# Retention in 192-token steps of three 64-token blocks, each block with its own running state

## The chip, the cores and the metric

One core of one Trainium2 chip. The metric is the device time of one launch in microseconds (us); the median of several runs counts.

## The reference

Attention without softmax and with a decay (retention), then a two-layer network. Batch 8 ("entries"), 8 heads, 576 tokens, head width 64; network width 512, hidden width 2048.

```python
scores = scale * np.matmul(q, k.transpose(0, 1, 3, 2))
gamma = 1.0 - 2.0 ** (-5.0 - np.arange(H))
Dmat = np.where(rel >= 0, gamma[:, None, None] ** rel[None, :, :], 0.0)   # rel = i - j
attn = np.matmul(scores * Dmat, v)
x = attn.transpose(0, 2, 1, 3).reshape(B * S, H * D)                     # 4608 x 512
h = x @ w_in
out = (h * (1.0 / (1.0 + np.exp(-1.702 * h)))) @ w_out
```

The decay factors into a power by the key's position, multiplied into v (`scale_v`), and one by the query's position (`gq`, applied when a result leaves PSUM). So a block of tokens needs three products: **scores** of its queries with its own keys, masked and multiplied with v (**values**); its keys with v, a 64x64 matrix for each head that is added to a running sum (**state**); and its queries with the sum of all earlier blocks (**inter**).

## The kernel before, in words

Each engine has one queue, written out by hand: `R.op` records operations in program order, and every operation waits for the last one that wrote or read the same buffer on another engine. Nothing is moved at run time, so an operation that waits holds up all that stand behind it in its queue.

**Dense work.** The 4608 tokens are 9 chunks of 512. `hidden(c, f)` is the first layer: four matmuls of 128x512 into one PSUM bank, then ACT applies the activation and writes `gT`. `project(c, r, g, bank)` is a quarter of the second layer for 128 tokens: four matmuls of 128x512; after the fourth quarter (g = 3) the bank is copied to `osb` by DVE (in chunk 0 by ACT) and stored by SP. Such a group of four matmuls is called a unit here. `hidden_half` is a unit of eight matmuls of 128x256. From chunk 3 on, `region(c)` alternates units of `hidden(c)` and `project(c - 1)`.

**Retention.** Entry 0 has a special path at the start. Entries 1 to 7 go in steps of 128 tokens (five in an entry, the last of 64). `burst(n)` puts one step between two units: PE computes values, state and inter of step n - 1 and, between their two parts, the scores of step n; then DVE masks the scores (`mask_s`, L426), moves the result to `xT` (`evac_o`, L573), and adds the state in `zacc` and casts it to `zq` (`evac_z`, L547 to L554), which the next burst reads. All these matmuls use quarters of the array: 64 rows and 64 columns, so four run at a time. The second part (`part(1)`) waits for PE's own first part (`own=first`).

**Inputs.** POOL issues loads in the order written (`load`, `load_entry`); k and v of heads 4 to 7 are shifted by 64 tokens (`load_shifted`). Three entries have room. `scale_v` on DVE multiplies v in place. q and k are turned (head width to partitions): steps up to 9 by PE and ACT (`turn`: eight transposes into bank `psW`, then `evac_t`), later ones by DMA transposes that SP issues three steps ahead (`dma_turn`), in one queue with the output stores.

**PSUM, eight banks.** `psS` two banks for scores; `psV` two banks for values, inter and state; `psW` for turns, and later for every second projection; `psU` for the other projections; `psH` two banks for `hidden`.

## Time and profile before

| what | value |
|---|---|
| runs (median; lowest, highest) | 307.18 us; 306.03, 308.02 |
| profiled execution, first to last instruction | 304.7 us |
| TensorE (PE) busy | 297.3 us, 98% |
| VectorE (DVE), ScalarE (ACT), GpSimd (POOL) busy | 147.8, 108.8, 154.2 us |
| granted TensorE clock | 1.00 |
| PE matmuls | 3175 recorded |

A launch takes about 2.5 us more than the span from first to last instruction (307.18 against 304.7). Busy shares are unions over each engine's instructions; PE's matmuls are pipelined, so the busy share says where PE has work and not that it runs at its peak.

### The profile page before, as it was taken

The page shows a single profiled execution, that of the slowest core. Times are in us where ns is not written, and L with a number is a line of the kernel's source. Part 1 is how long each engine was busy: PE and PEld are TensorE (multiplying, and loading weights), DVE is VectorE, ACT ScalarE, POOL GpSimd, SP SyncE. Part 2 cuts the span into 40 slices and gives each one's busy share as a digit, 9 for nine tenths or more (in the row PEclk, how much of TensorE's full clock was granted, in tenths as well). Part 3 has the DMA queues.
Part 4 walks back from the last instruction along what each step waited for, and adds up shares of the span by engine and source line. Part 5 has one row for each costly group of instructions (what it writes and reads, how often), then busy time and mean ns, then how long its engine had stood idle before and what let it go on. Part 6 is the DMA issues. An engine that isn't in the chain of part 4 may idle for free.

```text
span 304.7 us, 7234 instructions
## 1 busy us (share of the span) xinstructions
PE 297.3 (98%) x3175; PEld 151.0 (50%) x3175; DVE 147.8 (48%) x246; ACT 108.8 (36%) x183; POOL 154.2 (51%) x208
## 2 busy tenths in 40 slices
PE   7899999999999999999999999999999999999996
PEld 3454545885444444444444444444444444444444
DVE  6689837554767833545546433444364431100012
ACT  8666524661035423322333223323233333333300
POOL 8998999999999999999850000000000000000000
PEclk9999999999999999999999999999999999999999
DMA  9999999999999999999999933213231000001012
GB/s 69 152 195 196 176 168 200 155 145 129 158 194 175 132 156 164 169 161 173 174 169 163 133 84 95 58 38 86 71 80 37 34 37 34 34 37 66 37 54 86
DMA packets 154303, 35.61 MB, mean 117 GB/s; under 512 B 144928, under 2 KB 149792, under 8 KB 154272
## 3 DMA queue, kind: packets, MB, share of 16 engines
q0 software_dynamic: 118384, 18.36, 87.3%
q1 hardware_dynamic: 35888, 16.79, 29.3%
q8 instruction: 25, 0.41, 0.6%
q14 instruction: 6, 0.05, 0.1%
HBM read 36.70 MB, written 9.44 MB: 151 GB/s over the span
## 4 chain that ended last, share of the span: by engine, by line
PE 83%; POOL 9%; DMA 3%; DVE 3%; issue 1%; POOLq 0%
PE psH L634 31%; PE psU L687 18%; PE psW L687 16%; PE psV L445 4%; DMA st_k<-in_k_dram 3%; PE psH L687 3%; PE psH L671 3%; POOL st_k L211 2%; POOL st_q L198 2%; PE psS L404 2%; PE psU L671 1%; PE psV L464 1%; POOL st_k L198 1%; POOL st_v L198 1%; PE psV L457 1%; POOL st_v L211 1%
## 5 line engine op out<-in xcount | busy, mean ns | idle before, releaser
L639 ACT ACTIVATE gT<-psH 128x512 bf16<-128x512 f32 x121 | 72.2, 597 | 153.8 <-PE psH L634 153.8
L634 PE MATMUL psH<-xT,w_in_sb 128*128 128x512 bf16 x484 | 118.1, 379 | 0.0
L426 DVE TENSOR_TENSOR sm<-psS,mask 128x1024 bf16<-128x1024 f32 (+1 forms) x39 | 43.5, 1114 | 85.1 <-PE psS L404 80.8
L634 PEld LDWEIGHTS psH<-xT,w_in_sb 128*128 128x128 bf16 x484 | 45.8, 98 | 54.9 <-ACT gT L639 1.6
L211 POOL DMA_DIRECT2D st_k<-in_k_dram x70 | 69.2, 1250 | 1.6 <-PE psV L464 0.9
L211 POOL DMA_DIRECT2D st_v<-in_v_dram x70 | 68.1, 1240 | 0.0
L687 PE MATMUL psU<-w_out_sb,gT 128*128 128x512 bf16 x256 | 62.7, 379 | 0.0
L687 PE MATMUL psW<-w_out_sb,gT 128*128 128x512 bf16 x224 | 54.8, 379 | 0.0
L198 POOL DMA_DIRECT2D st_q<-in_q_dram x40 | 52.7, 1317 | 0.2 <-issue 0.2
L687 PEld LDWEIGHTS psU<-w_out_sb,gT 128*128 128x128 bf16 x256 | 24.2, 98 | 28.0
L687 PEld LDWEIGHTS psW<-w_out_sb,gT 128*128 128x128 bf16 x224 | 21.3, 98 | 25.0
L343 DVE TENSOR_TENSOR st_v<-st_v,vfac 128x512 bf16<-128x512 bf16 x37 | 25.2, 680 | 3.1 <-DMA st_v<-in_v_dram 3.1
L699 DVE COPY osb<-psU 128x512 f32<-128x512 f32 x15 | 10.3, 687 | 28.6 <-PE psU L687 28.6
L573 DVE TENSOR_TENSOR xT<-psV,gq 128x512 bf16<-128x512 f32 (+1 forms) x35 | 21.9, 627 | 4.2 <-PE psV L464 4.2
L699 DVE COPY osb<-psW 128x512 f32<-128x512 f32 x14 | 9.6, 689 | 21.7 <-PE psW L687 21.7
L687 PE MATMUL psH<-w_out_sb,gT 128*128 128x512 bf16 x80 | 18.7, 379 | 0.0
L445 PE MATMUL psV<-sm,st_v 64*64 64x64 bf16 (+1 forms) x504 | 17.5, 214 | 0.3
L445 PEld LDWEIGHTS psV<-sm,st_v 64*64 64x64 bf16 x504 | 9.1, 104 | 15.7 <-issue 12.1
L372 ACT ACTIVATE qk<-psW 128x1024 bf16<-128x1024 bf16 x10 | 10.2, 1023 | 9.2 <-PE psW L366 9.2
L457 PE MATMUL psV<-st_v,st_k 64*64 64x64 bf16 x448 | 13.0, 192 | 0.0
L464 PE MATMUL psV<-qk,zq 64*64 64x128 bf16 (+1 forms) x224 | 12.6, 215 | 0.1
L687 PEld LDWEIGHTS psH<-w_out_sb,gT 128*128 128x128 bf16 x80 | 7.6, 98 | 8.5
(108 smaller groups left out, 212.7 us busy)
## 6 DMA issues: line engine op xcount, KB each, us to landing
out_dram<-osb SPq DMA_DIRECT2D x35, 256.0 KB, 2.4
st_q<-in_q_dram POOLq DMA_DIRECT2D x32, 128.0 KB, 17.5
st_k<-in_k_dram POOLq DMA_DIRECT2D x57, 64.0 KB, 17.2
st_v<-in_v_dram POOLq DMA_DIRECT2D x57, 64.0 KB, 17.2
w_out_sb<-in_moe_w_out_dram POOLq DMA_DIRECT2D x4, 512.0 KB, 11.9
w_in_sb<-in_moe_w_in_dram POOLq DMA_DIRECT2D x3, 512.0 KB, 7.8
st_k<-in_k_dram POOLq DMA_DIRECT2D x4, 128.0 KB, 4.2
st_v<-in_v_dram POOLq DMA_DIRECT2D x4, 128.0 KB, 4.6
```

Source lines behind the costliest of these rows:

```text
L198: R.op("POOL", lambda e, d=d, s=s: e.dma_start(d, s), w=[(nm, sl, c)], dma=(nm, sl, c))
L211: R.op("POOL", lambda e: [e.dma_start(d, s) for d, s in parts], w=[(nm, sl, c)], dma=(nm, sl, c), parts=2)
L343: R.op(eng, lambda e: e.tensor_tensor(t, t, f, ALU.mult), r=[("vfac", min(b, 1))], w=[("v", sl, c)])
L426: R.op("DVE", lambda e: e.tensor_tensor(o, i, m, ALU.mult), r=[("mask", 0), ("mask", 1)] if b else mask3_keys if c == 3 else [("mask", 0)] ...
L445: i = e.matmul(psV[half(t), u, 128 * j + 64 * last : 128 * j + N], st_v[rows, sl, cc, 64 * h : 64 * h + 64], s[rows, j, 2 * t + u, 64 * la ...
L457: i = e.matmul(psV[half(j), u, 256 + 64 * t : 320 + 64 * t], st_k[rows, sl, cc, hs], st_v[rows, sl, cc, hs], start=False, stop=False, skip ...
L464: i = e.matmul(psV[half(t), u, 128 * j : 128 * j + N], zq[(c - 1) % 2][half(j), 2 * u + t, :], qk[n % NQK][half(j), 0, 2 * u + t, 0:N], st ...
L573: R.op("DVE", lambda e: e.tensor_tensor(xT[:, :, t0 : t0 + N].rearrange("p (u j) n -> p u j n", u=2), psV[:, :, 0:256].rearrange("p u (j n ...
L634: i = e.matmul(bank.ap(), w_in_sb[:, a, 128 * f : 128 * f + 128], xT[:, a, 512 * c : 512 * c + 512], start=(a == 0), stop=(a == 3))
L639: R.op("ACT", lambda e: e.activation(gT[c % 2][:, f, :], bank.ap(), AF.Gelu_apprx_sigmoid), w=[("gT", c % 2, f)], ps=[key])
L687: i = e.matmul(bank, gT[c % 2][:, f, 128 * r : 128 * r + 128], w_out_sb[:, f, :], start=(f == 0), stop=(f == NF - 1))
L699: R.op("DVE", lambda e: e.tensor_copy(osb[m].ap(), bank), w=[("osb", m)], ps=[key])
```

## The change

Entries 1 to 7 now go in steps of 192 tokens, three in an entry, m = 0 to 20 (entry 1 + m//3). A step is three blocks g of 64 tokens, and each block has a running state of its own (`zw[g]`). So no scores between different blocks are computed within a step: scores, values, state and inter are all products of 64 by 64 by 64, eight for each block and kind (no inter in an entry's first block, no state in its last).

- `burst(m_out, m_in)` does values and inter of step m_out and state and scores of step m_in. Its order on PE: phase_x (values of even blocks, half of inter), state of blocks 1 and 0, scores, state of block 2, phase_y (the rest). One wait on PE's own earlier work is kept in it.
- On DVE: `evac_wide` (768 elements), `mask_wide` (768), the state sums one block after the other (`state_wide`: 256 elements for an even block, two of 128 for an odd one), and one cast of all three to `zw`.
- PSUM: the five banks `psA` hold scores and parts of the state (0, 1), values and inter and parts of the state (2, 3), and turns and parts of the state (4, the former `psW`). The projections lose `psW`: they use `psU` alone in the regions.
- k is turned together with q of the same chunk; the first keys' own turn is gone. `qk` has six buffers instead of four, and SP turns six chunks ahead.
- Loads: k is no longer loaded a chunk ahead of q; the third and fourth parts of `w_out` stand at other places; entry b + 3 is loaded chunk by chunk as the steps of entry b finish.
- The order of units and bursts from the first projection to chunk 3 is written anew; in the regions a burst stands behind the second unit of a group of eight.

```diff
+            def score(e):
+                for blk, g in enumerate(blocks(m_in)):
+                    for t in range(2):
+                        for u in range(2):
+                            c, r = place(g, u)
...
+                            for j in range(2):
+                                i = e.matmul(psA[half(r), j, 64 * x : 64 * x + 64],
+                                             qk[n % NQK][half(j), 1, 2 * u + t, half(r)],
+                                             q_of(m_in, g, j, u, t), ...
...
+            if m_out is not None:
+                ro = [("sm", si(m_out)), "zw"] + [("v", b % NST, c) for c in cs] + queries(m_out)
...
+                done = R.op("PE", phase_x, r=ro, ps=["O", "Z"])
+            if m_in is not None:
...
+                before = R.op("PE", state_a, r=rs, ps=["S", "Z", "W"])
+                R.op("PE", score, r=rq, ps=["S"])
+                if m_in % 3 < 2:
+                    R.op("PE", lambda e: state(e, 2, (2,) if fresh else ()), r=rs,
+                         ps=["O", "W"], own=None if fresh else before)
+                    done = None
+                else:
+                    done = done and before
+            if m_out is not None:
...
+                R.op("PE", phase_y, r=ro, ps=["O", "Z"], own=done)
+                evac_wide(m_out)
+            if m_in is not None:
+                mask_wide(m_in)
+                state_wide(m_in)
...
+        def state_wide(m):
+            keys = ["S", "W", "Z", "O"]
...
+                if g % 2 == 0:
...
+                    add(src, blk, 0, 256, g == 0)
+                else:
+                    add(flat[:, at0 : at0 + 128], blk, 0, 128, False)
+                    add(flat[:, at1 : at1 + 128], blk, 128, 256, False)
+            R.op("DVE", lambda e: e.tensor_copy(z, zacc[:, 0 : len(gs), :]),
+                 r=[("zacc", x) for x in range(len(gs))], w=["zw"])
...
-        load(1, 0, "kq")
-        load(1, 1, "k")
+        load(1, 0)
         load_w_out(2)
-        load(1, 0, "v")
+        load(1, 1, "qk")
         load_w_out(3)
-        load_entry(1, 1)
+        load(1, 1, "v")
+        load_entry(1, 2)
         load_entry(2)
...
+        def step(m, into=True):
+            b, i = 1 + m // 3, m % 3
+            burst(m, m + 1 if into and m + 1 < NWIDE else None)
+            for c in ((0,), (1, 2), (3, 4))[i]:
+                n = NC * b + c + NQK
+                if PE_TURNS <= n < NSTEP:
+                    turn_dma(n)
+                if b + NST < B:
+                    load(b + NST, c)
+
+        def scale(m):
+            for c in ((0, 1), (2, 3), (4,))[m % 3]:
+                scale_v(NC * (1 + m // 3) + c)
...
+        run([unit_o(0, r, g, wide_banks[(1, 2, 0)[r]], "ACT") for g in range(4) for r in range(3)]
+            + [unit_o(0, 3, g, wide_banks[1], "ACT") for g in range(4)],
+            {1: [(tail_turn,)], 3: [(intra, 4)], 5: [(tail_out,)], 6: [(turn, 5)],
+             8: [(scale_v, 5)], 12: [(turn, 6), (scale_v, 6)], 14: [(burst, None, 0)]})
+        step(0, False)
+        turn_dma(10)
         hcount[0] = 16
+        run([unit_h(1, 0, f) for f in range(0, NF, 2)],
+            {0: [(turn, 7), (scale_v, 7)], 2: [(turn, 8), (scale_v, 8)],
+             5: [(burst, None, 1)], 6: [(turn, 9), (scale_v, 9)]})
+        run([unit_o(1, r, g, wide_banks[(1, 2)[r]]) for r in range(2) for g in range(4)],
+            {0: [(step, 1)], 4: [(step, 2, False)], 5: [(scale, 3)]})
+        run([unit_h(1, 1, f) for f in range(0, NF, 2)],
+            {3: [(burst, None, 3)], 5: [(scale, 4)]})
+        run([unit_o(1, r, g, wide_banks[(0, 1)[r - 2]]) for r in range(2, 4) for g in range(4)],
+            {1: [(step, 3)], 3: [(scale, 5)], 5: [(step, 4)]})
+        hcount[0] = 0
+        run([lambda f=f: hidden(2, f, 3) for f in range(NF)],
+            {1: [(scale, 6)], 3: [(step, 5)], 5: [(scale, 7)], 8: [(step, 6)],
+             10: [(scale, 8)], 13: [(step, 7)]})
...
+        hcount[0] = 0
+        scale(9)
         for c in range(3, NCH):
             region(c)
```

`run(units, between)` records the units in order, and behind unit i what `between[i]` names. `wide_banks` are psU, psH0, psH1 and a bank of psA, in this order; `hidden` rotates over psH0, psH1 and, with a third argument of 3, psU. In the new `region` each group of eight units is two hidden, four projections and two hidden in the order h0, o0, o1, h1, o2, o3, h2, h3; a burst follows o0, and `scale` follows h2.

## The prediction

> **What bounds the kernel now.** I read the page's head first, then its chain of waits.

> ```profile
> span 304.7 us, 7234 instructions
> ...
> PE 297.3 (98%) x3175; PEld 151.0 (50%) x3175; DVE 147.8 (48%) x246; ACT 108.8 (36%) x183; POOL 154.2 (51%) x208
> ...
> PE 83%; POOL 9%; DMA 3%; DVE 3%; issue 1%; POOLq 0%
> ```

> PE sets the end; the POOL and DMA shares lie before 47 us, where loads come in. So I count PE: work taken off it counts in full, and so does every new wait in its queue. A span of 304.7 belongs to a time of about 307.2, so 2.5 us lie around it, and I leave these as they are. A measurement here tells 1% (3.1 us) from no change.

> The timeline of PE around one steady burst (start, duration, line, shape, count) prices PE's work:

> ```profile
> 206.38 1.03 PE L634 MATMUL psH<-xT,w_in_sb 128*128 128x512 bf16 x4
> 207.34 0.31 PE L445 MATMUL psV<-sm,st_v 64*64 64x128 bf16 x8
> 207.48 0.23 PE L457 MATMUL psV<-st_v,st_k 64*64 64x64 bf16 x8
> 207.54 0.23 PE L464 MATMUL psV<-qk,zq 64*64 64x128 bf16 x4
> 207.59 0.34 PE L404 MATMUL psS<-qk 64*64 64x128 bf16 x16
> 207.84 0.26 PE L445 MATMUL psV<-sm,st_v 64*64 64x64 bf16 x8
> 207.92 0.23 PE L457 MATMUL psV<-st_v,st_k 64*64 64x64 bf16 x8
> 207.99 0.23 PE L464 MATMUL psV<-qk,zq 64*64 64x128 bf16 x4
> 208.15 0.39 PE L687 MATMUL psW<-w_out_sb,gT 128*128 128x512 bf16 x1
> ```

> Starts count, since durations overlap. A unit takes 0.864, so the burst could begin at 207.24 and holds PE until 208.15: 0.90. Eight 64-wide matmuls (L457) take 0.06: four run at once, 0.030 a round. A 128-wide round takes 0.055. Around the rounds lie 0.09 going in, 0.025 more after a start or wait, and 0.12 going out beyond the last round. The wait on PE's own part 1 ends about 0.28 after that part's last start.

> VectorE's operations by shape (count | busy, mean ns) price the other side:

> ```profile
> L426 DVE TENSOR_TENSOR sm<-psS,mask 128x1024 bf16<-128x1024 f32 x31 | 37.9, 1223 | 69.5 <-PE psS L404 65.9 <-PE psS L393 3.6
> L343 DVE TENSOR_TENSOR st_v<-st_v,vfac 128x512 bf16<-128x512 bf16 x37 | 25.2, 680 | 3.1 <-DMA st_v<-in_v_dram 3.1
> L573 DVE TENSOR_TENSOR xT<-psV,gq 128x512 bf16<-128x512 f32 x28 | 19.0, 680 | 0.0
> ...
> L552 DVE CAST zq<-zacc 128x256 bf16<-128x256 f32 x21 | 8.0, 380 | 0.7
> L549 DVE TENSOR_TENSOR zacc<-zacc,psV 128x256 f32<-128x256 f32 x14 | 5.7, 409 | 0.0
> ```

> Size sets them: 0.15 plus 1.04 ns an element. So 768 elements take 0.95 and 128 take 0.28. The cast's undisturbed duration is 0.293; for 768 I take 0.55, between that and three times it. An independent operation starts 0.09 before the one ahead ends, a dependent one 0.04 after. DVE starts 0.26 after PE's last start, and PE 0.06 after DVE's end: a `scale_v` that began at 44.78 and took 0.69 let the burst start at 45.53.

> **Part by part: PE's work.** Taken gap by gap between units, PE's small matmuls and its waits from the first projection (32.36) to the end sum to 34.2, 1.6 of it waits for loads. An entry's five bursts cost 0.79 + 0.90 + 0.90 + 0.90 + 0.61 = 4.1.

> After, a full burst has 6 rounds of values, 6 of scores, 6 of inter (4 if m_out is an entry's first step) and 6 of state (4 if m_in is its last): 22 rounds where m_out is the first or second step, 24 where it is the third. That is 0.09 + 22 x 0.030 + 0.05 + 0.07 (what the scores don't hide of the own wait) + 0.12 = 0.99, or 1.05. Eighteen such bursts: 13 x 0.99 + 5 x 1.05 = 18.1. The order breaks three joints: `burst(None, m)` for 0, 1 and 3 has 12 rounds (0.60 each, 1.8); `burst(m, None)` for 0, 2 and 20 has nothing to hide the own wait, 0.81 + 0.88 + 0.88 = 2.6. Turns 4 to 9 at 0.45, and the tail's scores (0.32) and values (0.48) as now: 3.5. Sum 26.0 against 34.2: **a gain of 8.2**. Units are the same in number. A longer run of 64-wide rounds than four has no row; its bounds are 0.028 (the closest pair) and 0.053 (a first pair after a stop). I take 0.030, by the unbroken pairs.

> [...]

> **Part by part: new waits of PE.** DVE's chain from a burst, where each operation depends on the last: mask 0.87, state sums 0.45 for an even block (256) and 0.64 for an odd one (2 x 128), cast 0.55: 2.96 after an entry's first step, 3.15 after its second, 2.4 after its third (two blocks). With `evac_wide` ahead 0.86 more: 3.8 to 4.0. PE must read `zw` at the next phase_x. In a region 6.9 of units lie between, and nothing waits. Between 32 and 113 us it is otherwise:

> - *Loads.* The third `w_out` part lands when it did, but its project comes 1.0 earlier: 0.2. The fourth now stands behind all of q and k of chunk 1 and lands about 1.1 later than its 42.1 (the trace's landing time); PE wants it at 42.0: 1.2. Together 1.4.
> - *burst(0, None)* has one unit (0.86) between it and step 0's scores, whose chain needs 2.96 + 0.3: 2.2 of wait. Hidden there before by three units and more.
> - *hidden_half(1)* then needs that burst's `evac_wide`: 0.26 + 0.95 + 0.06, less the usual exit: 1.1.
> - *turn(9)* writes `psW`, where parts of step 1's state lie, so it waits for DVE's last sum: ready 3.3 after `burst(None, 1)` began, PE there at 1.5: 1.8.
> - *step(4)* comes 3.45 after step 3, whose chain takes 4.0; then the copy of `osb` and `scale_v` of the last chunk (0.6 each) stand in DVE's queue ahead of what its state needs: 1.7.
> - *hidden(2, 0)* takes psH0, which the projection just finished; its copy stands behind step 4's chain (3.24) and the 0.69 of its own: PE is ready 1.7 after the burst, the bank 4.0: 2.3.
> - *steps 6 and 7* wait for `scale_v` behind the chain: 0.6 + 0.2. *hidden_half(1, 1)*'s second bank: 0.1.
> - *hidden(3, 0)* takes psH0 straight after hidden(2, 15) used it, so the activation (597 ns by L639) shows: 0.8.
> - *DMA turns.* These land 7 to 9 us after issue (page: 7.2 and 7.6 in the median). SP issues chunks 22 and 23 only after step 7 and q's landing at 113.7; step 9 wants them near 123, step 8 chunk 21 near 115: 1.4, bounds 0 and 3.

> Sum **13.6**. What stands behind these waits in other queues doesn't reach PE: the loads of entries 5 to 7 land about 10 us or more ahead of need by the landing times of before, and `osb` has three buffers for SP's stores.

> Net 13.6 - 8.2 = +5.4: span 310.1, time **312.6**.

> **The rivals.**

> *A. VectorE's chain is much shorter (not slower).* If the sums and the cast overlap more than rows of 256 and above show, five waits shrink together: burst(0, None), turn(9), step 4, psH0 and step 6, each by what the chain loses. So 1 us off every chain is worth some 4.5 to 5, and past 1.1 us the change wins: at 1.3 us the time is 306.7. For: L552's shortest, and the 128-wide sums have no row. Against: L426, L573 and L549 lie on one line to 1%.

> *B. More waits of the same kind.* The new order has some thirty places where PE waits for DVE or a DMA; two more of 1.2, or casts disturbed as L552's mean against 0.293 shows, give 315.2. For: L552 took 0.5 to 0.78 six times between 97 and 142. Against: regions have slack of 2 us and more.

> *C. Rounds paced by weight loads.* At 0.053 a round, 23 ns x 20 rounds x 21 steps = 9.7 more: 322. For: first pairs. Against: all unbroken ones. [...]

> *D. The change wins outright.* If PE waits nowhere for DVE, 8.2 less 2.8 for loads and turns: 301.8. Against it: each wait above follows from an operation's place in its queue.

> **How the numbers follow.** Forecast (309 to 314.5) 0.56, A 0.18, B 0.16, C 0.06, D 0.04. The range reaches down to where A ends the change's loss, 306.5, leaving out D and a part of A, and up to 317.5, leaving out C and little of B. Faster by over 1% (under 304.1): D and A's tail, 0.05. Within 1% (to 310.3): the rest of A and the lower edge of the forecast, 0.19. Slower: 0.76.

> **What would show it.** Right: a steady burst at about 1.0 with three in an entry; PE idle before `burst(0, None)`, turn(9), step 4 and hidden(2, 0), put down to DVE; the regions from chunk 3 shorter by some 4.7 (17.9 of bursts against 13.2), the stretch ahead of them longer by about 10. Wrong: steady bursts over 1.2 (C), chains under 3 us with `evac_wide` (A), or PE waits in the regions.

## The result and the profile after

The change makes the kernel slower: 318.41 us against 307.02 in runs on the same chip, a ratio of 1.0357 (1.0312 to 1.0401). The direction is as forecast; the size is twice the forecast 5.4 and the time lies 0.9 above the upper end of the range.

| | before | after |
|---|---|---|
| median (lowest, highest), us | 307.02 (306.03, 308.02) | 318.41 (316.45, 319.01) |
| profiled execution: time, span | 307.18, 304.7 | 318.88, 316.6 |
| the last 832 large weight loads (the regions, from behind chunk 3's first step on), first to last | 193.2 | 188.8 |
| start of the first of these loads | 108.5 | 124.8 |
| mean granted clock | 1.00 | 0.984 |

The rows on weight loads are read from the trace: large means 128x128, and both kernels have 832 of them from these points on. The regions are 4.4 shorter, close to the forecast 4.7. The stretch ahead, which has step 8 in it, is 16.3 longer where 10.1 was forecast. The whole error lies there.

The page of the changed kernel, head and chain:

```profile
span 316.6 us, 7664 instructions
...
PE 292.9 (93%) x3358; PEld 149.1 (47%) x3395; DVE 148.8 (47%) x274; ACT 108.3 (34%) x182; POOL 155.5 (49%) x208
...
PEclk9999998799997999999999999999999999999999
...
PE 76%; DVE 11%; DMA 5%; POOL 4%; issue 3%; POOLq 0%
```

PE's share fell from 98% to 93%, and DVE took 11% of the chain where it had 3%: new waits on DVE. Nothing in this says why the clock has two dips (slices 7, 8 and 13 of 40, each 7.9 us), nor what "issue 3%" is, which was 1%.

The chain of DVE was forecast well. Its groups by shape (count | busy, mean ns | idle before):

```profile
L623 DVE TENSOR_TENSOR xT<-psA,gq 128x768 bf16<-128x768 f32 x21 | 20.1, 958 | 52.9 <-PE psA L552 52.9
L634 DVE TENSOR_TENSOR sm<-psA,maskw 128x768 bf16<-128x768 f32 x21 | 19.9, 949 | 16.7 <-PE psA L564 16.7
...
L647 DVE TENSOR_TENSOR zacc<-zacc,psA 128x128 f32<-128x128 f32 x56 | 16.0, 286 | 1.7
...
L663 DVE CAST zw<-zacc 128x768 bf16<-128x768 f32 x14 | 8.5, 611 | 0.5
```

958 and 949 ns answer to the 0.95 used, 286 to 0.28, and 611 to 0.55. The timeline of PE around one steady burst of 22 rounds (start, duration, line, shape, count):

```profile
198.00 1.03 PE L730 MATMUL psU<-w_out_sb,gT 128*128 128x512 bf16 x4
198.96 0.32 PE L536 MATMUL psA<-sm,st_v 64*64 64x64 bf16 x16
...
199.35 0.38 PE L578 MATMUL psA<-qk 64*64 64x64 bf16 x24
...
199.71 0.23 PE L552 MATMUL psA<-qk,zw 64*64 64x64 bf16 x8
...
200.10 0.81 PE L730 MATMUL psU<-w_out_sb,gT 128*128 128x512 bf16 x3 [0.16 <-issue]
```

Here is a trap. From 198.86, where the unit ends, to 200.10 are 1.24 us. But the unit that follows shows x3: its first matmul has no record. Its weight loads are all in the trace. With the 0.216 of that matmul taken off, the burst costs 1.02 us; over the regions the mean is 1.013. Likewise a burst of 24 rounds reads 1.393 and costs 1.177. The "issue" gaps of 0.16 to 0.22 after bursts (2.2 us for psU L730 below) are such holes and no wait: 37 matmuls lack a record.

PE's waits (engine, buffer, line <- what ended the wait: us in all, times, longest):

```profile
PE psA L536 <- DVE zw L663: 2.8, 2, 2.2
PE psA L578 <- issue: 2.5, 2, 1.8
PE psU L730 <- issue: 2.2, 14, 0.2
PE psH L677 <- DVE osb L742: 2.1, 1, 2.1
...
PE psA L365 <- DVE zacc L647: 1.6, 1, 1.6
...
PE psH L714 <- DVE xT L623: 1.1, 1, 1.1
```

They are the forecast ones: step 0 and step 6 (L536: 2.2 and 0.6), `hidden(2, 0)` behind the copy of `osb` (L677), `turn(9)` behind the state sums (L365), `hidden_half(1)` behind `evac_wide` (L714). One is not: L578, the scores, stopped twice for 2.5 in all with nothing to release it.

Term by term, measured gap by gap between units of PE:

| term of the sum | forecast | measured |
|---|---|---|
| gain of bursts, turns and tail | -8.2 | -7.3 |
| loads of `w_out` | 1.4 | 0.6 |
| `burst(0, None)`, step 0 and `hidden_half(1)` | 3.3 | 3.3 |
| `turn(9)` | 1.8 | 1.8 |
| step 4 | 1.7 | 1.7 |
| `hidden(2, 0)` | 2.3 | 2.3 |
| steps 6 and 7, `scale_v` | 0.8 | 0.8 |
| `hidden(3, 0)`, second half bank | 0.9 | 1.0 |
| DMA turns | 1.4 | 0.1 |
| halved clock | none | 4.6 |
| stops inside steps 7 and 8 | none | 2.9 |
| net | +5.4 | +11.8 |

The last number stands against 11.9 between the spans. Six rows of waits agree to 0.1. Two rows that the sum lacked are 7.5 together, and make the miss. Of the other errors, 0.9 too much gain and 2.1 too much for loads and turns partly cancel, which is luck.

### The profile page after: what moved, and what is told of

It reads as the page before. It is cut to its first block, busy times and chain, and to the rows that moved or that the text cites. A ratio compares the mean times of both kernels' runs of the same rounds, so it can differ in the third digit from the quotient of the medians.

```text
span 316.6 us, 7664 instructions
## 1 busy us (share of the span) xinstructions
PE 292.9 (93%) x3358; PEld 149.1 (47%) x3395; DVE 148.8 (47%) x274; ACT 108.3 (34%) x182; POOL 155.5 (49%) x208
## 4 chain that ended last, share of the span: by engine, by line
PE 76%; DVE 11%; DMA 5%; POOL 4%; issue 3%; POOLq 0%
PE psU L730 28%; PE psH L677 27%; PE psH L730 6%; DMA w_out_sb<-in_moe_w_out_dram 4%; PE psH L714 3%; DVE zacc L647 3%; PE psA L536 2%; PE psA L578 2%; DVE sm L634 2%; DVE xT L623 2%; PE psU L714 2%; DMA st_k<-in_k_dram 2%; PE psA L564 1%; POOL st_q L208 1%; PE psA L552 1%
## 5 line engine op out<-in xcount | busy, mean ns | idle before, releaser
L677 PE MATMUL psH<-xT,w_in_sb 128*128 128x512 bf16 x453 | 110.3, 383 | 3.7 <-DVE osb L742 2.1
L730 PE MATMUL psU<-w_out_sb,gT 128*128 128x512 bf16 x416 | 100.9, 379 | 2.3 <-issue 2.2
L677 PEld LDWEIGHTS psH<-xT,w_in_sb 128*128 128x128 bf16 x464 | 43.5, 98 | 60.2 <-ACT gT L682 7.3
L730 PEld LDWEIGHTS psU<-w_out_sb,gT 128*128 128x128 bf16 x432 | 41.1, 98 | 47.8
L742 DVE COPY osb<-psU 128x512 f32<-128x512 f32 x26 | 17.9, 688 | 72.4 <-PE psU L730 72.4
L623 DVE TENSOR_TENSOR xT<-psA,gq 128x768 bf16<-128x768 f32 x21 | 20.1, 958 | 52.9 <-PE psA L552 52.9
L730 PE MATMUL psH<-w_out_sb,gT 128*128 128x512 bf16 x120 | 28.7, 379 | 1.4 <-issue 0.8
L634 DVE TENSOR_TENSOR sm<-psA,maskw 128x768 bf16<-128x768 f32 x21 | 19.9, 949 | 16.7 <-PE psA L564 16.7
L647 DVE TENSOR_TENSOR zacc<-zacc,psA 128x128 f32<-128x128 f32 (+1 forms) x77 | 24.8, 322 | 2.2
L730 PEld LDWEIGHTS psH<-w_out_sb,gT 128*128 128x128 bf16 x128 | 11.9, 98 | 14.0 <-DMA w_out_sb<-in_moe_w_out_dram 0.9
L536 PE MATMUL psA<-sm,st_v 64*64 64x64 bf16 x504 | 11.9, 197 | 3.0 <-DVE zw L663 2.8
L371 ACT ACTIVATE qk<-psA 128x1024 bf16<-128x1024 bf16 x10 | 10.2, 1023 | 11.7 <-PE psA L365 11.7
L714 PE MATMUL psH<-xT,w_in_sb 128*128 128x256 bf16 x88 | 12.8, 298 | 1.1 <-DVE xT L623 1.1
L536 PEld LDWEIGHTS psA<-sm,st_v 64*64 64x64 bf16 x504 | 7.6, 107 | 12.4 <-issue 6.8
L663 DVE CAST zw<-zacc 128x768 bf16<-128x768 f32 (+1 forms) x21 | 11.6, 550 | 0.7
## 6 DMA issues: line engine op xcount, KB each, us to landing
st_k<-in_k_dram POOLq DMA_DIRECT2D x57, 64.0 KB, 11.6
```

The source lines that it names most:

```text
L536: i = e.matmul(psA[half(t), 2 + u, at : at + 64], rows_of(st_v, m_out, g, u, 4 * u + 2 * t + j), smw[si(m_out)][half(r), j, 2 * blk + t, : ...
L623: R.op("DVE", lambda e: e.tensor_tensor(xT[:, :, t0 : t0 + 192].rearrange("p (u j) n -> p u j n", u=2), psA[:, 2:4, 0:384].rearrange("p u ...
L634: R.op("DVE", lambda e: e.tensor_tensor(o, i, k, ALU.mult), r=["maskw"], w=[("sm", si(m))], ps=["S"])
L647: R.op("DVE", lambda e: e.tensor_tensor(to, was, src, ALU.add), r=[("zacc", (blk - 1) % 3)], w=[("zacc", blk)], ps=keys)
L677: i = e.matmul(bank.ap(), w_in_sb[:, a, 128 * f : 128 * f + 128], xT[:, a, 512 * c : 512 * c + 512], start=(a == 0), stop=(a == 3))
L714: m = e.matmul(bank[:, 256 * i : 256 * i + 256], w_in_sb[:, a, 128 * (f + i) : 128 * (f + i) + 128], xT[:, a, a0 : a0 + 256], start=(a == ...
```

## Two theories

**K, the clock.** The trace's windows of PE, cut at the times at which the granted clock changes (window, its length, PE busy (count), clock, DMA share, GB/s):

```profile
49.41:52.82 3.41, 1.03 (x42) 1.00 1.79 242
52.82:56.23 3.41, 2.45 (x16) 0.50 2.12 196
...
93.78:97.19 3.41, 1.27 (x7) 1.00 1.79 142
97.19:100.61 3.42, 3.42 (x10) 0.50 1.64 186
```

All changes stand on one grid of 3.413 us. In the window before each fall PE was busy for only 1.03 and 1.27 us (2.38 and 2.14 idle): the waits at step 0 and at `hidden(2, 0)`. The next window runs at 0.50, and a 128x512 matmul takes 0.427 there instead of 0.216. A halved window loses 1.71 us where PE works through all of it. In the first of the three windows PE stood for 0.96, so the three lose 4.6, matmul by matmul. The four runs of the changed kernel fit: clocks of 0.984, 0.989, 0.995 and 0.984 went with spans of 316.6, 315.3, 314.5 and 316.9, so three, two, one and three windows, some 1.1 for each window more. K says: a window with enough idle time in it halves the next.

**F, the program.** The stop inside step 8, in the timeline:

```profile
120.78 0.35 PE L578 MATMUL psA<-qk 64*64 64x64 bf16 x20
122.90 0.22 PE L578 MATMUL psA<-qk 64*64 64x64 bf16 x4 [1.77 <-issue]
```

The scores stop after 20 of 24, in the middle of one operation whose inputs all came together. Counting PE's instructions in the trace (a matmul is two, a weight load and a matmul; an instruction that only waits for a semaphore is one), the two stops stand behind instruction 2754 and 3010, 256 apart. The trace has a queue q8, "instruction", with 16 KB packets at 112.54 to 113.79 and 120.07 to 121.24; PE went on 1.5 and 1.7 after their ends. F says: PE's program arrives in blocks of 256 instructions, a block comes some 7 us after the one before was entered while POOL's loads run (entered at 108.46, 115.26 and 122.90: 6.8 and 7.6 apart), and PE stops where it is faster. A burst of 22 rounds is 176 instructions in 0.8 us; before, 112. The trace has 6854 instructions of PE instead of 6405.

The rivals to K and F stand in the expectations.

## Experiments on the clock

**e4_idle**: the kernel before with stalls in it, each a chain of dependent copies on DVE that PE waits for; nothing else changes.

```diff
+        def stall(count):
+            last = R.q["PE"][-1]
+            for _ in range(count):
+                R.op("DVE", lambda e: e.tensor_copy(
+                    posi[:, 0:2, :], psS[:, 0, 0:2, :]),
+                    w=["stall"], ps=["S"], own=last)
...
+        stalls = {(7, 5): 4, (7, 13): 5, (7, 21): 4, (7, 29): 5,
+                  (8, 2): 3, (8, 10): 4, (8, 18): 5, (8, 26): 6}
...
+                if g == 1:
+                    stall((7, 5, 4)[r])
```

`stalls` gives the region, the unit in it and the number of copies; the last two lines are for the tail, and every large unit now waits for "stall".

> The kernel before, with eleven places between 240 and 310 us at which PE waits for a chain of 3 to 7 dependent copies on VectorE (256 elements each), so for an estimated 1.7, 2.1, 2.6, 3.1 or 3.5 us; the work is the same otherwise. Theory K: a grid of 3.41 us windows runs on its own; the clock falls to 0.50 at the end of a window of which PE was idle for some 2.5 us or more, and stays for one window if PE is then busy. So waits of 1.7 never do it, waits of 2.1 and 2.6 only where they lie inside one window, and 3.1 and 3.5 about half the time or more; every stretch at 0.50 is a multiple of 3.41 us and starts on the grid. Rival L: no fall at all, since nothing else is loaded there. Rival M: the length of the single wait decides (over 2.2 us always, below never).

The span was 345.3 and the mean clock 0.965. Two of the places, windows of PE:

```profile
258.84:262.25 3.41, 2.34 (x11) 1.00 0.00 0
262.25:265.66 3.41, 1.99 (x10) 1.00 0.20 77
...
296.38:299.80 3.42, 1.14 (x6) 1.00 0.00 0
299.80:303.21 3.41, 3.19 (x9) 0.50 0.00 0
```

A wait of 2.5 us from 260.6 on fell on both sides of a window's edge, 1.07 and 1.42 of idle, and the clock stayed. The third row had 2.28 idle in one window (3.42 less 1.14), and the next window ran at 0.50. So the length of the wait did not decide here, 2.5 without a fall, but its share of one window, 2.28 with one. Over the traces of all kernels of this study the clock fell 20 times while PE still had work. The window before had 2.06 to 3.41 us in which PE neither multiplied nor loaded weights, and no window with 1.93 or less was followed by a fall. The clock came back after windows with 0.53 or less, and not after those with 0.83 or more. So K stands, with a lower limit than the 2.5 that it was given, and the rivals L and M fall.

**e1_fill**: the changed kernel with 34 matmuls on a spent operand put into five of its waits; 94 small matmuls at the start shift the program's blocks.

```diff
-        fill(14)
...
+        small(94)
+        fill(11)
...
+        fill(9, *wide_banks[0])
         step(0, False)
+        fill(4, *wide_banks[0])
...
-             5: [(burst, None, 1)], 6: [(turn, 9), (scale_v, 9)]})
+             5: [(burst, None, 1)], 6: [(fill, 7, *wide_banks[0]), (turn, 9), (scale_v, 9)]})
...
-            {1: [(step, 3)], 3: [(scale, 5)], 5: [(step, 4)]})
+            {1: [(step, 3)], 3: [(scale, 5)], 5: [(fill, 5, *wide_banks[2]), (step, 4)]})
+        fill(9, *wide_banks[2])
```

> The changed kernel, with matmuls on zeros (34 of 128x512, 0.216 us each) put into PE's five longest waits between 49 and 97 us: 9 before step 0, 4 behind it, 7 before turn(9), 5 before step 4, 9 before hidden(2, 0). The waits themselves stay. At the start 3 of 14 such matmuls are replaced by 94 small ones, so that the later instructions keep their places in blocks of 256. Theory K: the 5.1 us that the halved clock took (three stretches of 3.41 us at 0.50) come from PE's idleness in these waits; the clock stays at 1.00, the span falls from 316.6 to about 311.5 and the time by 3 to 5 us. Rival L: the clock falls for another reason, such as the load of all engines and transfers together at these places; 0.50 shows again and the time stays within 1 us or grows.

The clock was 1.000 and the time did not move: 318.15, ratio 1.0351 (1.0306 to 1.0395). So K is right on what halves the clock, and wrong that curing it gains 3 to 5 us here. Of the 4.6, 4.2 came back as other delays, gap by gap: 2.0 at step 2 (1.5 of it a new stop, from 73.06 to 74.54), 0.6 of longer waiting at step 0, 0.7 of small matmuls at the start, 0.6 of waits ahead of 43 us, 0.3 at step 4. Part of this is F's.

## Experiments on the program's blocks

**e7_code**: the kernel before with 640 small matmuls ahead of region 3, while loads run, and 640 behind region 8, when they are over.

```diff
+        small(640, (psH[0], psH[1]), [("H", 0), ("H", 1)])
         for c in range(3, NCH):
             region(c)
+        small(640, (psH[0], psH[1]), [("H", 0), ("H", 1)])
```

> The kernel before, with two runs of 640 small matmuls on zeros (64 by 64 by 64, four at a time, 1280 instructions of PE each): one ahead of chunk 3's region at about 108 us, while the loads run, and one behind the last region at about 302 us, where only the output's stores are left. At 0.0317 us a round of four each run takes 5.1 us. Theory F: PE gets its program in blocks of 256 instructions, one asked for when the one before is begun. At 108 us each block needs 6.8 to 7.6 us, so the run takes some 30 to 38 us with a gap of 6 us or so at every 256th instruction; at 302 us, with fetches of 1 us and 1.5 behind them, 2.5 to 2.8 a block and 12 to 14 us in all. Rival T: no gaps, 5 to 6 us each, and the same in both places.

The timeline of both places (128 small matmuls are 256 instructions):

```profile
114.96 1.92 PE L899 MATMUL psH<-idle 64*64 64x64 bf16 x128 [6.44 <-issue]
121.98 1.92 PE L899 MATMUL psH<-idle 64*64 64x64 bf16 x128 [5.10 <-issue]
...
331.26 1.93 PE L899 MATMUL psH<-idle 64*64 64x64 bf16 x128 [2.77 <-issue]
334.72 1.92 PE L899 MATMUL psH<-idle 64*64 64x64 bf16 x128 [1.53 <-issue]
```

128 matmuls take 1.9 us in five of these blocks and 1.2 in the one at 327.26 (the mean clock of the run was 0.947), and then PE stands for 5.1 to 6.4 us early and 1.5 to 2.8 late. A block takes 7.0 to 8.1 us while the loads run and 3.2 to 4.0 when they are over, more than the 2.5 to 2.8 expected there. F stands: this is the cost of a block measured by itself.

**e2_shift**: the changed kernel with 62 small matmuls for two large ones at the start, so that every later block ends 120 instructions earlier in the work.

```diff
-        fill(14)
...
+        small(62)
+        fill(12)
```

> The changed kernel with 62 small matmuls on zeros at its start in place of 2 of 14 large ones, where PE only keeps busy: every later PE instruction lies about 120 places further in the program, nothing else differs. Theory F: the stalls inside the scores of steps 7 and 8 (0.91 and 1.96 us) are waits for the next block of 256 instructions, which in the changed kernel are 256 places apart and each end some 1.5 us after a 16 KB packet of the instruction queue. With block ends 120 places earlier in the code these fall among whole units, and both stalls go: the span is 2.5 to 2.9 us shorter if the clock does what it did. Rival T: those stalls are the scores' own, waiting for DMA turns of chunks 19 to 21; they stay where they are, and so does the time.

The timeline, at step 1 and at step 8:

```profile
70.58 0.22 PE L536 MATMUL psA<-sm,st_v 64*64 64x64 bf16 x3 [1.32 <-issue]
...
122.23 0.38 PE L578 MATMUL psA<-qk 64*64 64x64 bf16 x24
```

Step 8's scores are whole now; with step 7's they give 2.9 back. A new stop came inside step 1, behind instruction 1474, which is 5 x 256 ahead of 2754. That the stops of steps 7 and 8 go was forecast, the sum was not: with the new stop, 0.7 more at step 4 and 1.0 lost by 43 us, most of it to the small matmuls, the time is 318.54, ratio 1.0374 (1.0325 to 1.0423). A shift of the blocks moves the stops.

**e9_no_loads**: the changed kernel without the loads of entries 4 to 7.

```diff
-                if b + NST < B:
+                if b + NST < 4:
```

> The changed kernel without the loads of entries 4 to 7 (POOL's issues from about 85 to 160 us): those entries are computed from the data of entries 1 to 3, the order and number of all other operations stay. Theory F, with the loads as what makes PE's code late: from some 95 us on the blocks of 256 instructions come in 3 to 4 us as they do at the end of the kernel, the stalls inside the scores of steps 7 and 8 (0.9 and 1.9) are gone, and nothing else on PE gets longer: span some 2.8 below 316.6, or below what the granted clock of this run makes of it. If the delay comes from the fetches themselves, or from the DMA turns, which stay, the blocks still take 7 us and the stalls remain.

One execution took 313.33, with a span of 311.3 and a clock of 0.995. Step 8 in the timeline:

```profile
117.58 0.38 PE L578 MATMUL psA<-qk 64*64 64x64 bf16 x24
```

Both stops are gone with the program as it was: steps 7 and 8 cost 1.24 and 1.18, and PE entered blocks 5.7 us apart without a stop. The packets of these two blocks began 0.7 and 0.9 us after the block before was entered; in the changed kernel it was 4.1 and 4.8. So what the loads delay is the start of the packet, and the stops come from the loads and the density of bursts together; the DMA turns, which stay, are not the cause. One window was halved instead of three, 1.7 lost instead of 4.6. These two, 2.9 and 2.9, less 0.5 that this run was behind before the first wait already, are the 5.3 between the spans.

## Experiments on the order

These keep the change and write its order anew, to take away the waits of the table. Numbers stand for "behind unit i", as in the change.

**e5_order**: eight buffers for `qk`, turns and `scale_v` earlier, `hidden(2, 0)` begins in psH1.

```diff
-NQK = 6
+NQK = 8
...
-            {0: [(turn, 7), (scale_v, 7)], 2: [(turn, 8), (scale_v, 8)],
-             5: [(burst, None, 1)], 6: [(turn, 9), (scale_v, 9)]})
+            {1: [(turn, 8), (scale_v, 8)], 3: [(turn, 9)],
+             5: [(burst, None, 1)], 6: [(scale_v, 9)]})
...
-            {3: [(burst, None, 3)], 5: [(scale, 4)]})
+            {2: [(burst, None, 3)], 4: [(scale, 5)], 5: [(scale, 6)]})
...
-        hcount[0] = 0
+        hcount[0] = 1
```

> The changed kernel with its steps and the bursts' work as they are, but another order between 40 and 125 us and eight buffers qk: burst(None, 0) two units earlier, turn(7) ahead of the first half unit, turn(9) ahead of burst(None, 1), step 3 one unit earlier, scale_v of the later steps ahead of the chains, hidden(2, f) beginning with psH1. By the prediction's terms this takes away most of burst(0, None) (1.7 of 2.2), 0.45 of the half unit's 1.1, turn(9)'s 1.8, step 4's 1.7, hidden(2, 0)'s 2.3, hidden(3, 0)'s 0.9 and step 6's 0.6: 9.4 us, and by theory K the clock stays at 1.00, 5.1 more. Theory F sets a bound: with the steps closer together, each block of 256 instructions still takes 6.8 to 7.6 us to come while the loads run, so stalls of 1 to 4 us show at block ends in steps 5 to 8. Sum: span 303 to 306, time about 305 to 308.5, as fast as before. Without F 302 or less; if the waits only move elsewhere, 312 or more.

312.96, ratio 1.018 (1.0131 to 1.023). The waits of `turn(9)`, `hidden(2, 0)` and `hidden(3, 0)` are gone. My order had a fault of its own: `scale(6)` waited in DVE's queue for a v that landed at 84.4, and step 4 behind it waited 2.5. Block ends took 1.0 and 2.6 in steps 7 and 8.

**e6_order2**: steps earlier still, so that each has units on both sides.

```diff
-             8: [(scale_v, 5)], 12: [(turn, 6), (scale_v, 6)], 14: [(burst, None, 0)]})
-        step(0, False)
...
+             8: [(turn, 6), (scale_v, 6)], 10: [(burst, None, 0)], 14: [(step, 0, False)]})
...
-            {0: [(step, 1)], 4: [(step, 2, False)], 5: [(scale, 3)]})
+            {1: [(step, 1)], 5: [(step, 2)], 6: [(scale, 4)]})
...
-            {1: [(step, 3)], 3: [(scale, 5)], 5: [(step, 4)]})
+            {2: [(step, 4)], 4: [(scale, 6)]})
```

> The changed kernel with the same steps and bursts, but the order between 38 and 130 us drawn up by three rules: no step sooner than four units after the one whose state it needs, no scale_v whose data have not landed ahead of a chain, and at least six units between steps 3 to 8, so that 256 instructions of PE take about 7 us. The fourth part of w_out is loaded before chunk 1 of entry 1, step 2 becomes a full burst, hidden(2, f) begins with psH1, step 8 stands behind the fifth unit of its group, qk has eight buffers. By the terms that the traces bore out, it loses 0.6 (w_out), 3.3 (step 0 and the half unit behind it), 1.8 (turn(9)), 1.7 (step 4), 0.8 (steps 6 and 7), 3.2 (psH0, twice), 0.5 (a burst less), 5.1 (clock, theory K) and 2.8 (stalls at block ends, theory F): 316.6 less 19.8, so a span of 296.8, or up to 300 where some block ends still stall: time 299 to 302.5, faster than before by 1.3 to 2.5%. If theory F is wrong, and the stalls in the scores of steps 7 and 8 belong to those steps, 2.8 more; if K is wrong, 3 to 5 more.

313.91, ratio 1.0229 (1.0201 to 1.0256), far above what I expected. Four units had to wait behind a copy of `osb`, 3.5 once and 3.3 together in the three other places. From 79.8 to 116.6 PE entered its blocks 7.1 to 7.6 us apart; at the last three it came 1.4 to 1.7 us after their packets had ended and had stood for 2.1 in all, so there the program paced it.

**e8_order3**: one of the copies of `osb` on ACT, steps 3 to 5 and those of chunk 3 moved again.

```diff
-        run([unit_o(1, r, g, wide_banks[(1, 2)[r]]) for r in range(2) for g in range(4)],
-            {0: [(step, 1)], 4: [(step, 2, False)], 5: [(scale, 3)]})
+        run([unit_o(1, r, g, wide_banks[(1, 2)[r]], ("DVE", "ACT")[r])
+             for r in range(2) for g in range(4)],
+            {1: [(step, 1)], 5: [(step, 2)], 6: [(scale, 4)]})
```

> The reordered kernel e6_order2 with its own three new waits mended: the copy of chunk 1's second quarter on ScalarE, so that hidden_half(1, 1) doesn't find psH1 behind step 2's chain (3.5, and 1.7 of clock with it); chunk 3's steps behind the seventh unit of a group, so that the copy of osb stands ahead of the chain (1.0 + 1.7 + 0.6); turn(6) one unit later (0.9 of 1.3). Steps 3 to 7 lie six to seven units apart. Theory F: PE then runs from about 75 to 125 us at the rate of its code, 7.1 to 7.6 us for 256 instructions, with stalls of 1 to 2.5 in all, and not below. Span 301.5 to 303.5, time 303.8 to 306: 0 to 1% faster than before. If code supply is no bound, 300 or less.

309.95, ratio 1.0086 (1.0054 to 1.0118). The `osb` waits are gone. One block end fell inside step 3 and stopped PE for 2.5; in the same step the scores waited 0.9 for a DMA turn, which landed at 77.12, 0.06 ahead of them. That idle time halved the clock behind it (mean 0.989). The two theories meet: the clock fell here behind a stop for the program as it did elsewhere behind waits for DVE.

**e10_order4** (steps 3 to 6 one or two units later than in e8_order3) and **e11_order4_shift** (the same with 62 small matmuls at the start).

```diff
-            {3: [(burst, None, 3)], 5: [(scale, 4)]})
+            {4: [(step, 3)], 6: [(scale, 5)]})
...
-            {1: [(step, 3)], 3: [(scale, 5)], 5: [(step, 4)]})
+            {2: [(step, 4)], 5: [(scale, 6)]})
```

> e8_order3 with step 3 two units later, and steps 4, 5 and 6 one unit later: in e8_order3 one block of code ended inside step 3, 8.6 us after the one before it, and PE stood there for 2.5 and 0.9 us, after which the clock halved for two windows (4.0). Theories F and K: with two more units ahead of step 3 the block has 10 us, the stall and the halving go: 307.5 less 7.4 is a span of 300.1, or up to 302 where a block end stalls elsewhere; time 302.5 to 304.5, faster than before by 0.8 to 1.5%. If the stall belongs to step 3 itself (its sums, its data), it moves with the step and the time stays at 308 to 310.

> e10_order4 with 62 small matmuls on zeros at the start in place of 2 of 14 large ones, which cost some 0.6 us there: the same work with the block ends 120 instructions earlier in the code. Theory F: the stalls fall at other steps; the sum of PE's stalls at block ends differs from that of e10_order4 by up to 3 us in either direction, all of them at places 256 apart, and nothing else differs but the 0.6. If block ends don't matter, the time is that of e10_order4 plus 0.6, within 0.5 us.

e10_order4: 308.86, ratio 1.0064 (1.0036 to 1.0092), profiled with a clock of 1.000. No wait of PE for DVE over 0.5 is left; yet the span is 306.3 and not the 300 to 302 expected. Two bounds are left in this stretch. Blocks still end inside four steps. One of these stops in the timeline:

```profile
89.86 0.26 PE L552 MATMUL psA<-qk,zw 64*64 64x64 bf16 x10
91.02 0.22 PE L552 MATMUL psA<-qk,zw 64*64 64x64 bf16 x2 [0.90 <-issue]
```

The four cost 3.3 (0.6, 1.2, 1.1 and 0.4), at places 256 apart. Another 4.0 was lost right in front of scores (PE's waits: us in all, times, longest):

```profile
PE psA L578 <- issue: 1.9, 2, 1.3
PE psA L578 <- DMA qk<-st_k: 1.7, 2, 1.0
```

None of these four stops is at a block's end, and each ended 0.04 to 0.06 us after a DMA turn had landed (67.79, 76.32, 99.98 and 124.49). They are waits for turns, the two under "issue" too. The next expectations still count most of both kinds as block ends, 6.8 together, and that reading is wrong.

The shift moved the block ends to other steps (2.7 and 2.8 at steps 1 and 2, others at 3 to 5), where they cost 8.3 in all. PE, later by this, found its turns landed, and no scores waited. The time went to 310.19, ratio 1.0106 (1.0071 to 1.0141), 1.3 more, 0.9 of it there by 43 us. So where a block ends does matter, and the two bounds hide each other: time saved on the one is in part waited for at the other.

**e12_spread**: fewer instructions per us. Chunk 2's projections stand ahead of chunk 3's hidden units, and steps 7 to 10 among them, eight units apart.

```diff
+        run([unit_o(2, r, g, wide_banks[(0, 1, 2, 0)[r]]) for r in range(4) for g in range(4)]
+            + [lambda f=f: hidden(3, f, 3) for f in range(NF)],
+            {8 * i + k: [(fn, 7 + i + d)] for i in range(4) for k, fn, d in ((3, step, 0), (5, scale, 2))})
...
-        for c in range(3, NCH):
+        for c in range(4, NCH):
```

> The steps spread out: chunk 2's sixteen projections now come ahead of all of chunk 3's hidden units, so that steps 3 to 10 can stand seven to eight units apart (e10_order4: six to seven); step 2 is without a step behind it again, step 3's first half a burst of its own. Same bursts, same units. In e10_order4 the clock was 1.00 and no wait for VectorE of over 0.5 us was left, but PE stood at a block's end in five steps, for 1.2 to 1.5 us each, 6.8 together. Theory F: with 240 instructions in some 7.9 us the code keeps up, so 5 to 6 of the 6.8 go, and 0.5 comes back for the burst more: span 300.5 to 302, time 303 to 305, faster than before by 0.7 to 1.3%. Rival: if those stops belong to the steps, the time stays at 308 to 310.

311.42, ratio 1.0109 (1.007 to 1.0147). The stops at block ends fell from 3.3 to 1.5, as F has it, and one wait of 1.5 for a turn was left (landed at 78.40, scores from 78.46). New: a unit of `hidden` waited 3.8 for psU behind a copy to `osb`, whose buffer was still being stored. SP had issued that store at 117.76, behind two turns, and it landed at 126.45. The wait halved the clock of one window too.

**e13_spread2**: turns six ahead, the copy of the last 128 rows of chunks 1 and 2 on ACT, `scale_v` later.

```diff
-                n = NC * b + c + NQK
+                n = NC * b + c + 6
...
+        run([unit_o(2, r, g, wide_banks[(0, 1, 2, 0)[r]], ("DVE", "DVE", "DVE", "ACT")[r])
...
+            {3: [(step, 7)], 6: [(scale, 9)], 10: [(step, 8)], 16: [(scale, 10)],
+             18: [(step, 9)], 23: [(scale, 11)], 25: [(step, 10)], 30: [(scale, 12)]})
```

> e12_spread with its own new waits mended. There, SP's queue held the output's stores behind DMA turns eight chunks ahead, whose data had not landed, so that VectorE waited for osb and PE for psU (4.0, and 1.7 of clock), and PE waited for psH0 behind a scale_v (1.5): now the turns go out six chunks ahead, the last quarter's copy of chunks 1 and 2 is on ScalarE, and scale_v stands later. Steps 3 and 8 to 10 are moved by a unit, which should spare the two stalls at block ends that were left (1.3 each). Theories K and F: clock 1.00, no block of code under 8 us between 68 and 165 us, span 310.6 less 7 to 9.8: 300.8 to 303.5, time 303 to 306, so 0.4 to 1.3% faster than before. Rival, that steps of this form cost more than their rounds whatever the spacing: 308 or more.

307.69, ratio 1.0011 (0.9984 to 1.0037): level with the kernel before. The profile has a clock of 1.000 and two block ends left, 1.1 and 0.4. The rest are waits of scores for DMA turns: those of steps 3, 6, 9 and 12 (0.4, 1.3, 1.1, 1.5). The second, in the timeline:

```profile
99.29 0.30 PE L564 MATMUL psA<-st_v,st_k 64*64 64x64 bf16 x16
100.69 0.38 PE L578 MATMUL psA<-qk 64*64 64x64 bf16 x24 [1.10 <-DMA qk<-st_k]
```

The turn's data landed at 100.64, 0.05 ahead of the scores' start (the idle before them reads 1.10; from start to start, less the work, it is 1.3). The other three waits end within 0.1 of a landing as well. SP had issued this turn at 93.11, straight behind that of the same chunk's q at 91.84, and this q had been loaded at 91.83. So an earlier place in SP's queue would not have helped; the loads and the 7.5 us of this turn (93.11 to 100.64) set it.

**e14_spread3**: turns seven ahead instead of six; turns 8 and 9, `burst(None, 1)` and step 1 one unit earlier, steps 9 and 10 one later.

```diff
-                n = NC * b + c + NQK
+                n = NC * b + c + 7
...
-            {0: [(turn, 7), (scale_v, 7)], 2: [(turn, 8), (scale_v, 8)],
-             5: [(burst, None, 1)], 6: [(turn, 9), (scale_v, 9)]})
+            {0: [(turn, 8), (scale_v, 8)], 2: [(turn, 9), (scale_v, 9)],
+             4: [(burst, None, 1)], 6: [(scale, 3)]})
```

> e13_spread2 with DMA turns seven chunks ahead instead of six, turn(8), turn(9), burst(None, 1) and step 1 a unit earlier, steps 9 and 10 a unit later. In e13_spread2 the clock was 1.00, one block end stalled (step 2, 1.1), and PE's other stops were scores waiting for a DMA turn (steps 6, 9 and 12: 1.3, 1.1 and 1.5 us, each ended within 0.1 us of a turn's landing). If those turns were late because they were issued late, 2 to 3 of the 3.9 go and 0.9 of step 2's: span 301.5 to 303, time 303.5 to 305.2, faster than before by 0.7 to 1.2%. If they were late because their data were (loads landing as POOL issues them), steps 9 and 12 wait as before and only 1 to 2 us go: 305 to 306.5, no change that can be told from before.

309.92, ratio 1.0066 (1.0035 to 1.0098): a miss. The profiled execution, span 309.9, is one of its longer ones (the shortest span was 304.3). In it the waits for turns grew, to 2.1 for the scores of step 6 and 3.3 for those of step 12, and two windows ran at half clock, which cost 3.3. The distance is no cure: the q that step 6 needs landed at 91.50, SP issued its turn at 91.52 and k's at 92.84, and this one landed at 101.22. The landing of the loads is the next bound. No version clearly beat the kernel before.

## Why the prediction was wrong in size

- **What bounds the kernel**: right. PE's queue set the end in all kernels, and time taken off it or put in counted in full.
- **PE's work**: the gain was 7.3, not 8.2. The mis-sized term is the five bursts that begin with a third step: 1.18 each instead of 1.05, since their scores follow the state 0.18 later where 0.07 to 0.08 is usual; why was not looked into. Bursts of 22 rounds cost 1.01 (0.99 forecast), those of 12 rounds 0.60 and those without scores 0.88, as forecast. Over runs of nine rounds and more a round takes 31.7 ns; the 0.030 taken from pairs was right. **C** falls with this: a first pair after a stop takes 52 ns here too (198.962 to 199.014), the rounds behind it don't.
- **New waits on DVE**: right, place by place and to 0.1. **A** falls: the operations are not shorter than forecast. **D** falls with it.
- **Loads and DMA turns**: too large, 0.7 measured against 2.8. The DMA turns' 1.4 was in truth 0.1; step 8's delay is not a turn but a block end.
- **The step that failed is the sum of the waits**: 13.6 was forecast and 11.6 of these came. It counted each wait at its length alone. Missing was what a wait does to the clock of the 3.4 us behind it (4.6), shown by e4_idle and e1_fill, and what 176 instructions in 0.8 us ask of the program's arrival (2.9), shown by e7_code and e9_no_loads. Both were left out without a reason.
- **B** had the nearest price, 315.2 (312.6 and two waits of 1.2 would be 315.0), and the wrong cause: there are no further waits for DVE of weight.

What stays open: e13_spread2 is 10.7 below the changed kernel, so nearly all of the loss is order, clock and program, and not in the bursts. But its span is still 0.7 above the kernel before, although bursts save 7.3. Of the 8.0 between, 1.5 (two block ends) and 4.3 (four turns) are named; the remaining 2.2 were not taken apart. Open as well is what the halved clock costs net: e1_fill took it away, and the time stayed.

## What to carry to other kernels

Work out for every wait of PE how much idle time it can put into one window of 3.41 us: by an estimate from the limits found here (2.06 us of idle or more in the window before a fall, 1.71 lost in one that is halved), two waits of 1.2 in one window cost up to 1.7 us more in the next, and the same two in different windows do not. Smaller matmuls buy work with instructions (176 in a burst here, 112 before), so before a change that adds many, divide PE's instructions by 256 and set the blocks against the time that each has, above all while loads run (in e7_code a block took 7.0 to 8.1 us then, and 3.2 to 4.0 when they were over). A stop that stands in the middle of one operation, after its first instructions went through, has no buffer or semaphore behind it here: look at the instruction queue before looking for a wait. A stop in front of an operation's first instruction is another matter, even where the profile says "issue": compare its end with the landings of DMAs.
